# A new order of steps in a one-core kernel of a long convolution beside a gated feed-forward layer

## The chip, the cores and the metric

The kernel runs on one core of a Trainium2 chip. The metric is the device time of one execution in microseconds, taken as the median of several runs. The core has five engines with a queue of instructions each: TensorE (PE in the profile, its weight loads PEld), VectorE (DVE), ScalarE (ACT), GpSimd (POOL) and SyncE (SP), which in this kernel issues nearly all transfers. Each queue runs in order. An instruction that has to wait for another engine or a transfer holds up everything behind it on its own queue.

## The reference

```python
x = A_q                                  # (1, 2048, 640), bf16
xn = _layernorm(x, axis=-1)
# A: short convolution with 4 taps, gate, long convolution over the whole sequence
k_shift = sum over t of k_pad[:, t:t + S, :] * shift_k[:, 3 - t]
kv = k_shift * v
y = irfft(rfft(kv, 4096) * rfft(ssm_k, 4096))[:S]     # along the sequence
y = y + kv * ssm_D
A = xn * y
# B: gated feed-forward, 640 -> 1728 -> 640
h = _sigmoid(xn @ w_gate) * (xn @ w_up)
B = h @ w_down
return x + A + B
```

## The kernel before

The 2048 positions are laid on 128 partitions with 16 blocks each; the 640 channels are 5 chunks of 128. Two independent jobs share the core.

The feed-forward goes over four groups t of 512 positions. In each group there are 14 slices fc of the hidden width: `gate_mm` and `up_mm` (line 260, five matmuls each) write a PSUM tile, `gate_ev` (ScalarE, line 269) takes the sigmoid, and `up_ev` (VectorE, line 275) multiplies and writes `hT`. The last half-wide slice does both halves at once (`both_mm`, `both_ev`, `both_mul`, lines 281 to 290). Then come 16 `down_mm` steps of seven matmuls (line 304), and eight `down_ev` (VectorE, line 309) that add the result to `x`. For groups 1 to 3 the input is normalised on VectorE (`ln_norms`, `ln_var`, `ln_xn`, lines 198 to 219), with the inverse root on GpSimd (`ln_pow`, line 214), and turned by four DMA transpositions `xn_turn` into `xnT` (line 240). `xnT` is one buffer: the turns of a group wait for the last product of the group before, and the first `gate_mm` of a group waits for the turns.

The long convolution is done per chunk c as a Fourier transform in two stages by matrix products. The filter is turned on VectorE by `h_turn` (line 323) and its first element gets D added on GpSimd by `add_D` (line 317), which reads the one small buffer `dr`. VectorE forms the four-tap convolution and the gate in 16 `kv_op` steps (lines 337 to 346). `st1_mm` (lines 363 and 365, eight steps a chunk) is the first stage; `st1_ev` copies its PSUM tile into one of two `t1` buffers (`t` in the profile), and `wr1` writes a full one to DRAM (line 377). `rd2` reads it back in another layout (line 387), and `st2_mm` (line 396), `st2_ev` and `prod` (lines 409 and 411) do the second stage and the product with the filter. `inv1_mm` (line 425), `inv1_ev`, `wr2` (lines 441 and 445), `rdb` (line 455) and `inv2_mm` (line 464) transform back, and `inv2_q` and `inv2_x` (lines 469 and 474) multiply by `xn` and add to `x`.

PSUM is split into two pools. Pool `psG` has four tiles for gate, up, down and inv2 results; pool `psC` has two larger ones for st1, st2 and inv1. A matmul step that takes a tile waits for the eviction of the tile that had the buffer four (or two) steps before. The evictions of st1, st2 and inv1 go to ScalarE, or to VectorE where the order says so by one of the letters F, J and I in place of B, C and A.

The loads are steps as well: `load_k` and `load_halo` fill one of two K buffers (`kx`, chunk c uses number c modulo 2; the halo is the three columns ahead of the first), `load_v` one of two `kvh` buffers, `load_h` the filter `hn` and D's row `dr` (one buffer each, so it waits for `h_turn` and `add_D` of the chunk before), `load_taps` and `taps` the tap table, `load_x` the input of a group.

What runs when is written out by hand. Each kind of step is a chain with a letter, in its own fixed order, and one string names the chains in the order of issue:

```python
    left = {k: iter(v) for k, v in chains.items()}
    for k in "".join(ORDER.split()):
        fn, args = next(left[{"F": "B", "J": "C", "I": "A", "Y": "E"}.get(k, k)])
        fn(*args, **({"copy": dve_copy} if k in "FJIY" else {}))
```

Each engine sees its instructions in the order of this string. The letters that matter here: m, n the first loads and TB table; g all matmuls of the feed-forward; s and u their evictions; a, A, w stage 1, its eviction and its write-out; r, b, B, p stage 2; c, C, W, R, d, q the way back; k the short convolution; h, K, V, T the loads of later chunks; H, D the filter; l, P, e the normalisation and the turns; o the stores. Steps are numbered from 0 in the order of the string, 845 in all.

Of the kernel before, what the change touches and what calls it, by code (L numbers as in the profile page):

```python
# [57 lines left out]
def kernel(  # L58
# [569 lines left out]
    step("o", store, NB - 1, NB, 4 * P, DM)  # L628

    ORDER = """  # L630
    mgmmmmgmgmgsummZmgmgsmmgugmssgkmmukgskgugkusgsugkkgkHggmmuskuggkHmssukgmDgggukskgukkksaTmmgauAgmkaAH
    HlglAalAlglmwgautAkagugmggPmwlkgAhglkelauleggkakukkugekAAuuDkHgkuaaekgkwgsATKugkAwgsnkkgskgtuKaKAuka
    gskkgauwgkAlDAakVgglkKkrsakAuwAgakgVsAgalswAkaguKgkkAurbgkBswksHgTBgkbtuguBBpkgawkgslaAgsuKkalupKgrA
    AgkahPlnHsAwugaglVasgkgVpAsTAKukDpuckwglkkCgaCaHAugkAkgkeklubkgrkBBgguuwkgbggkpghtBBrbkegleBgBaauegw
    HAparguVkApauAkgwpADWaugakksAngkugpkwlAsucgsgJlpkCulbrgBKBsgaAuapgpAgrbsFggBussWkukrlpcHgguPCCgbslkV
    ggBuBgbpslBkuBRdpgspgWqqcusdgCgkrkkrCsbqFugqBgubskgBRdwBuagpAaqAdgllWwrsewRpugaqgIaggrpAaAaqupgIqupg
    ddcCgeuqgJebgupegFRuBgqbBpgqBgWpdcrguqqgJqCrubwuwdrgFpBgsbqpggpWpqBugBpscsuJggCurpgbggRFBbsWpdsudupq
    rgBqgqBcqRJsgrpCgsbBuWguBpdspqgbuBBgpqdpsgcgrugCRJqbpggsduBqsBgupgspgWqRqcuJdqgsgCdoqgusqWgudggqgugo
    uRgquRggddouqqgguqddgqqqqoquqggoogouoogouoooo
    """  # L640
    left = {k: iter(v) for k, v in chains.items()}
    for k in "".join(ORDER.split()):
# [33 lines left out]
```

## Time and profile before

| | us |
|---|---|
| median of 3 runs | 238.9 (238.31 to 239.72) |
| the profiled execution | 237.94 |
| its span, first to last instruction | 236.2 |
| TensorE busy | 229.1 (97%) |
| VectorE busy | 204.1 (86%) |
| ScalarE busy | 121.7 (52%) |
| DMA queue of SP, share of 16 engines | 90.3% |

The granted TensorE clock is at full speed throughout. Busy time of a matmul runs from its start to a modelled end, and matmuls overlap, so the sum over a group is larger than the time it takes from TensorE; the time from one start to the next (the pitch) is what counts. In the lists of waits the columns are the engine and line that waited, what ended the wait, the total in us, the number of waits and the longest one. In a timeline row they are the start and the duration in us, then engine, line, operation, what is written and read, and in brackets the idle time of the engine before it.

### The profile page before, as it was taken

The numbers are of one execution on the slowest core, as the hardware profiler recorded it, in microseconds if no ns is written. First come the engines' busy times: TensorE is split into PE (matmuls) and PEld (weight loads), VectorE is DVE, ScalarE is ACT, GpSimd is POOL, SyncE is SP. The second block draws the span as 40 slices with busy tenths as digits, with TensorE's granted clock in tenths as the row PEclk, the third lists the DMA queues.
The fourth block names the chain that finished last, engine by engine and source line by source line (L and its number), as shares of the span: only waits on it lengthen the run. The fifth ranks groups of instructions, "written<-read, shape, count | busy, mean of one in ns | idle before, by whom it ended". The sixth has DMA issues, their size and how long they took to land.

```text
span 236.2 us, 5433 instructions
## 1 busy us (share of the span) xinstructions
PE 229.1 (97%) x2205; PEld 131.2 (56%) x2205; DVE 204.1 (86%) x364; ACT 121.7 (52%) x152; POOL 11.5 (5%) x24
## 2 busy tenths in 40 slices
PE   7799999999899899999999999999999999999995
PEld 3664445877355445666754444478664344446772
DVE  3632898999969999999999999899999999988473
ACT  2343323633564897776776777653346367653000
POOL 5210000020100001000100010000000000000000
PEclk9999999999999999999999999999999999999999
DMA  6999999958899999899899996899989879556664
GB/s 211 292 313 237 259 308 299 257 174 163 223 317 269 321 253 270 225 286 217 228 232 321 248 265 186 240 246 271 235 260 284 238 186 255 160 155 177 191 212 134
DMA packets 97183, 56.79 MB, mean 240 GB/s; under 512 B 55878, under 2 KB 91270, under 8 KB 96902
## 3 DMA queue, kind: packets, MB, share of 16 engines
q1 hardware_dynamic: 96214, 55.62, 90.3%
q10 hardware_dynamic: 944, 0.82, 1.1%
q8 instruction: 17, 0.28, 0.5%
q14 instruction: 8, 0.07, 0.1%
HBM read 36.12 MB, written 18.35 MB: 231 GB/s over the span
## 4 chain that ended last, share of the span: by engine, by line
PE 84%; DVE 8%; DMA 4%; issue 1%; ACT 0%; ACTq 0%; DVEq 0%
PE pg L260 23%; PE pu L260 23%; PE pd L304 20%; PE psb L464 4%; PE ps L396 3%; DMA w<-in_B_w_up_dram 3%; PE ps L363 3%; PE ps L365 3%; PE psa L425 2%; PE pg L281 1%; DVE st L198 1%; DVE tmp L341 1%; DMA xnT<-xn 1%; DVE acc L343 1%; PE pu L251 1%
## 5 line engine op out<-in xcount | busy, mean ns | idle before, releaser
L260 PEld LDWEIGHTS <-w 128*128 128x128 bf16 x500 | 46.5, 98 | 55.8 <-issue 6.8
L304 PE MATMUL pd<-wd,hT 128*128 128x320 bf16 (+2 forms) x448 | 65.3, 299 | 0.0
L260 PE MATMUL pg<-xnT,w 128*128 128x512 bf16 x250 | 62.2, 380 | 0.9 <-DMA xnT<-xn 0.9
L260 PE MATMUL pu<-xnT,w 128*128 128x512 bf16 x250 | 62.2, 380 | 0.8 <-DVE hT L275 0.8
L304 PEld LDWEIGHTS <-hT 128*128 128x128 bf16 x448 | 41.9, 98 | 18.2 <-issue 2.3
L223 ACT CAST t<-ps 128x1024 bf16<-128x1024 f32 x38 | 37.8, 1016 | 23.6 <-PE ps L365 16.0
L269 ACT ACTIVATE sig<-pg 128x512 bf16<-128x512 f32 x52 | 31.1, 603 | 30.7 <-PE pg L260 27.7
L223 ACT CAST xz<-ps 128x1024 bf16<-128x1024 f32 x35 | 34.2, 1015 | 20.3 <-PE ps L396 20.3
L275 DVE TENSOR_TENSOR hT<-sig,pu 128x512 bf16<-128x512 bf16 x52 | 34.8, 675 | 9.6 <-PE pu L260 5.6
L411 DVE TENSOR_TENSOR xz<-xz 128x2048 bf16<-128x2048 bf16 x20 | 24.3, 1215 | 0.1
L365 PE MATMUL ps<-kvh,S1t 128*128 128x128 bf16 x160 | 21.7, 220 | 0.0
L363 PE MATMUL ps<-kvh,S1t 128*128 128x128 bf16 x160 | 21.6, 218 | 0.0
L341 DVE TENSOR_TENSOR tmp<-kx,sc 128x1024 bf16<-128x1024 bf16 x30 | 20.5, 683 | 0.4
L343 DVE TENSOR_TENSOR acc<-acc,tmp 128x1024 bf16<-128x1024 bf16 x30 | 20.5, 684 | 0.4
L309 DVE TENSOR_TENSOR x<-pd,x 128x320 bf16<-128x320 f32 (+2 forms) x32 | 15.2, 483 | 5.9 <-PE pd L304 5.7
L363 PEld LDWEIGHTS <-S1t 128*128 128x128 bf16 x160 | 15.5, 97 | 2.8 <-DVE kvh L346 0.3
L365 PEld LDWEIGHTS <-S1t 128*128 128x128 bf16 x160 | 15.4, 96 | 2.6
L198 DVE BATCH_NORM_STATS2 st<-x 128x6 f32<-128x320 bf16 x32 | 13.9, 476 | 2.7 <-DMA x<-in_A_q_dram 2.7
L469 DVE TENSOR_TENSOR yx<-psb,xn 128x512 bf16<-128x512 f32 x20 | 13.7, 684 | 1.4 <-PE psb L464 1.0
L409 DVE STREAM_SHUFFLE xz<-xz 128x512 f32<-128x512 f32 x20 | 14.5, 725 | 0.0
L223 ACT CAST ao<-psa 128x1024 bf16<-128x1024 f32 x11 | 10.8, 1014 | 5.8 <-PE psa L425 5.6
L464 PEld LDWEIGHTS <-TBt 128*128 128x128 bf16 x160 | 9.8, 98 | 3.0 <-issue 1.5
(48 smaller groups left out, 149.3 us busy)
## 6 DMA issues: line engine op xcount, KB each, us to landing
d<-t SPq DMA_DIRECT2D x20, 512.0 KB, 5.3
t<-d SPq DMA_DIRECT2D x20, 512.0 KB, 5.7
bi<-d SPq DMA_DIRECT2D x8, 512.0 KB, 4.8
d<-ao SPq DMA_DIRECT2D x6, 512.0 KB, 5.6
kx<-in_A_k_dram SPq DMA_DIRECT2D x10, 256.0 KB, 5.3
hn<-in_A_ssm_k_dram SPq DMA_DIRECT2D x20, 128.0 KB, 5.2
kvh<-in_A_v_dram SPq DMA_DIRECT2D x10, 256.0 KB, 5.4
x<-in_A_q_dram SPq DMA_DIRECT2D x3, 640.0 KB, 6.4
```

What stands on the lines that cost most here:

```text
L198: nc.vector.bn_stats(d["st"][:, i, s2, :], x[:, b, s2 * 320:(s2 + 1) * 320])
L223: nc.scalar.copy(out=out, in_=in_)
L260: nc.tensor.matmul(pg[:, :], lhsT=w[:, c, u * UP + fc * P:u * UP + (fc + 1) * P], rhs=xnT[:, :, c, :], start=(c == 0), stop=(c == NC - 1))
L269: nc.scalar.activation(sig[fc][:, :], pgs[0, fc][:, :], ACT.Sigmoid)
L275: nc.vector.tensor_tensor(hT[:, fc, :], sig[fc][:, :], pgs[1, fc][:, :], ALU.mult)
L304: nc.tensor.matmul(pd[:, :], lhsT=hT[:, fc, bb * P:(bb + 1) * P], rhs=wd[:, fc, es], start=(fc == 0), stop=(fc == NFC - 1))
L341: nc.vector.tensor_tensor(d["tmp"][:, :, :], kx[:, lo + 3 - m:hi + 3 - m, :], sb(m), ALU.mult)
L343: nc.vector.tensor_tensor(d["acc"][:, :, :], d["acc"][:, :, :], d["tmp"][:, :, :], ALU.add)
L363: nc.tensor.matmul(ps[:, i, 0:P], lhsT=S1[:, b, h, :], rhs=cin[c]["kvh"][:, 0, b, :], start=True, stop=True)
L365: nc.tensor.matmul(ps[:, i, P:2 * P], lhsT=S1[:, b, h, :], rhs=hp[:, b // 2, b % 2, :], start=True, stop=True)
L411: nc.vector.tensor_tensor(z[:, 1:3, :, :], z[:, 0:1, :, :].to_broadcast((P, 2, 8, P)), z[:, 1:3, :, :], ALU.mult)
L464: nc.tensor.matmul(ps[:, i, :], lhsT=TB[:, h, 4 * m + i, :], rhs=bi[:, h, 4 * (m % 2) + i, :], start=(h == 0), stop=(h == 1))
```

## The change

Only the string ORDER is replaced. All chains and all functions stay, so the same 845 steps are issued, each chain in its own order; what moves is how the chains are woven into each other. Fifteen evictions change their engine: seven go from VectorE to ScalarE and eight the other way, so that VectorE has 15 of them (letters F, I and J) instead of 14.

```diff
     step("o", store, NB - 1, NB, 4 * P, DM)
 
     ORDER = """
-    mgmmmmgmgmgsummZmgmgsmmgugmssgkmmukgskgugkusgsugkkgkHggmmuskuggkHmssukgmDgggukskgukkksaTmmgauAgmkaAH
-    HlglAalAlglmwgautAkagugmggPmwlkgAhglkelauleggkakukkugekAAuuDkHgkuaaekgkwgsATKugkAwgsnkkgskgtuKaKAuka
-    gskkgauwgkAlDAakVgglkKkrsakAuwAgakgVsAgalswAkaguKgkkAurbgkBswksHgTBgkbtuguBBpkgawkgslaAgsuKkalupKgrA
-    AgkahPlnHsAwugaglVasgkgVpAsTAKukDpuckwglkkCgaCaHAugkAkgkeklubkgrkBBgguuwkgbggkpghtBBrbkegleBgBaauegw
-    HAparguVkApauAkgwpADWaugakksAngkugpkwlAsucgsgJlpkCulbrgBKBsgaAuapgpAgrbsFggBussWkukrlpcHgguPCCgbslkV
-    ggBuBgbpslBkuBRdpgspgWqqcusdgCgkrkkrCsbqFugqBgubskgBRdwBuagpAaqAdgllWwrsewRpugaqgIaggrpAaAaqupgIqupg
-    ddcCgeuqgJebgupegFRuBgqbBpgqBgWpdcrguqqgJqCrubwuwdrgFpBgsbqpggpWpqBugBpscsuJggCurpgbggRFBbsWpdsudupq
-    rgBqgqBcqRJsgrpCgsbBuWguBpdspqgbuBBgpqdpsgcgrugCRJqbpggsduBqsBgupgspgWqRqcuJdqgsgCdoqgusqWgudggqgugo
-    uRgquRggddouqqgguqddgqqqqoquqggoogouoogouoooo
+    mmmmmmmmmggggsmmsumggsguuZsgggmukksmgmskmukgkggkmuksHgsggumkuggskgukHgskgmkmuggmkTsksgKuugkDagaAgkmA
+    uaHKtHmwmagllllAglgDPkAuaAwmklllahuelgekAugekakkugaggAgkggkAakaukuewgkukmkkgsTggAkuwsngkVutAgaskwkgs
+    AKgaukgrHkaAgAualakswkgAagVguskrAgAbgkwTksuBkBskkguKDgskkHlkaagguAlAKkngbtwushungpkplBsBgaAwgaugkpKl
+    gksaupgAAPlglswkVslrgkuKaueaglHAwaggkkAAVDcwCggTkaCkukuaAgregHkkAbggkugBBKkuurpbBgeklgBkgpbpgBluBpeg
+    atawAkuWggskuaklpghuAwasgAAgaarluAkHrkggAcVskgkJupgsCbgDswBugkBuspaAaKklgPgpAbugBkFsWrgRkcVCCsgugpdH
+    rsbpBkgBugWqudbsgplkpgrBBcurgqRCsqJgbgWkwgukgswpBrBlubksBFqgusludapdqaglgeAaguggRqAeaquAwAappgAaepqe
+    ggIcgCuwguJbBgpFdgrbpqugWBuqdpqBrgcugJpqgrCbugpsRwBFggpbupgBdsrqBuWpgdqrcJspggqgCbuFRqBggsubpdsWugBB
+    gdprscCqgpJrqgbsuBgqFRgupsgbspudpgqrWBgBduqqRcpgJCqWgsqbsBugBgpugsRdpgpucsgqJqCWdgqgusqgudgqouggudRq
+    gqugoRogggqudguodqgqqdudoggqqqqgogqoouuoooooo
     """
     left = {k: iter(v) for k, v in chains.items()}
     for k in "".join(ORDER.split()):
```

Places of the steps that the prediction speaks of, counted in the string:

| step | before | after |
|---|---|---|
| h_turn(0,1) | 64 | 68 |
| load_halo(2) | 176 | 86 |
| wr1(0,0) | 112 | 107 |
| load_k(2,0,8) | 193 | 103 |
| add_D(1) | 159 | 119 |
| ln_pow(1) | 126 | 120 |
| load_h(2) | 133 | 133 |
| xn_turn(1,0) to (1,3) | 137, 142, 153, 167 | 135, 138, 143, 166 |
| gate_mm(1,0) | 169 | 168 |
| load_v(1,8,16) | 127 | 172 |
| kv_op(2,0) | 198 | 195 |
| wr1(1,1) | 229 | 220 |
| up_ev(1,4) | 228 | 228 |
| st2_mm(0) | 255 | 235 |
| load_x(3) | 307 | 270 |
| load of the TB table | 429 | 279 |
| wr1(3,1) | 416 | 421 |
| inv1_mm(1) | 441 | 441 |

## The prediction

> **What bounds the kernel now.** First the page, for shares; then TensorE's waits; then, for each wait, the timeline around it and the waits of the engine that ended it.
>
> ```profile
> span 236.2 us, 5433 instructions
> PE 229.1 (97%) x2205; PEld 131.2 (56%) x2205; DVE 204.1 (86%) x364; ACT 121.7 (52%) x152; POOL 11.5 (5%) x24
> ```
>
> TensorE's busy share is overstated, because matmuls overlap. So I measured pitches, start to start: 1.08 us for a gate or up product (5 matmuls), 0.95 for seven down matmuls, 0.45 for an st1 or inv2 group, 0.47 for st2, 0.69 for inv1. The ordered steps then add up to 216.2 us of TensorE work. The first starts at 14.39 us and the last at 232.73; the last costs 0.39. 232.73 + 0.39 - 14.39 = 218.7, so TensorE loses only about 2.5 us in the whole order, and all that counts is in two places.
>
> ```profile
> PE pg L260 <- DMA xnT<-xn: 0.9, 1, 0.9
> PE pu L260 <- DVE hT L275: 0.8, 1, 0.8
> ```
>
> By pitch these are 1.10 us (the st1 group at 58.51 + 0.45 = 58.95, next product at 60.05) and 0.93 us (gate_mm(1,6) at 75.72 + 1.08 = 76.80, up_mm(1,6) at 77.73): 2.03 us, or 0.85% of the span. That is the most an order alone can win on TensorE; VectorE, 97% busy from 80 to 200 us (116.6 of 120), hides beside it.
>
> The first wait, in the timeline (start, duration, engine, line, tiles):
>
> ```profile
> 48.80 0.17 DVE L210 TENSOR_SCALAR var<-mv 128x4 f32<-128x4 f32 x1
> 49.11 1.02 POOL L214 TENSOR_TENSOR rstd<-var,mhalf 128x4 f32<-128x4 f32 x1 [17.25 <-DVE var L210]
> 50.10 0.42 POOL L317 TENSOR_TENSOR kvh<-kvh,dr 1x128 bf16<-1x128 bf16 x1
> 50.55 0.26 SPq L136 DMA_DIRECT2D dr<-in_A_ssm_D_dram  x1
> 50.90 2.35 SPq L139 DMA_DIRECT2D hn<-in_A_ssm_k_dram  x4
> 53.36 5.27 SPq L240 DMA_TRANSPOSE xnT<-xn  x4
> 60.05 1.24 PE L260 MATMUL pg<-xnT,w 128*128 128x512 bf16 x5 [0.93 <-DMA xnT<-xn]
> ```
>
> The first normalised block is ready at 50.84, but its transposition is issued only at 53.36: SP stands at load_h(2), which overwrites dr and so waits for add_D(1), and add_D(1) stands on POOL behind ln_pow. SP's own waits, cut to 40 to 82 us, price it:
>
> ```profile
> SPq L136 <- POOL kvh L317: 3.3, 1, 3.3
> ```
>
> The second wait comes from VectorE, which had lost time ten microseconds earlier:
>
> ```profile
> 69.21 0.69 DVE L337 TENSOR_TENSOR acc<-kx,sc 128x1024 bf16<-128x1024 bf16 x1 [1.73 <-DMA kx<-in_A_k_dram]
> 76.99 0.68 DVE L275 TENSOR_TENSOR hT<-sig,pu 128x512 bf16<-128x512 bf16 x1
> 77.73 1.24 PE L260 MATMUL pu<-xnT,w 128*128 128x512 bf16 x5 [0.77 <-DVE hT L275]
> ```
>
> kv_op(2,0) waited 1.73 us for K of chunk 2, issued at 62.16. up_ev(1,4), which frees the PSUM buffer for up_mm(1,6), ran late behind it.
>
> **The change, part by part.** All instructions stay; one eviction more goes to VectorE (15 against 14). Work ahead of a step is counted in pitches: VectorE 0.60 for a conv or up step, 1.03 a statistics block, 0.36 a normalisation, 0.40 a down_ev, 1.14 an eviction; ScalarE 0.91 an eviction.
>
> First wait, credit 1.10. add_D(1) now stands ahead of ln_pow on POOL, so load_h(2) no longer waits for it. SP comes from wr1(0,1), which waits for st1_ev(0,3) (st1_mm(0,2) arrives at 44.9, then taps(1) and two evictions on ScalarE: about 47.6), then load_v(1,0,8) (0.4), then load_h(2) with its 2.35: SP is free near 51.5. Against this, h_turn(0,1) now stands behind up_ev(0,10) and kv_op(0,9) and ends at about 36.4 instead of 34.7; load_h(1) waits for it, its data land near 43.5 (5.3 after the last issue, as before), and h_turn(1,0) starts 0.8 later than its 42.68. So ln_var ends at 49.75 and rstd at 50.9. Three VectorE steps (0.6 + 0.4 + 0.6) stand between, so ln_xn(1,0) runs at 51.35 and the first transposition at 51.8, the fourth three pitches of 1.35 later: 55.85 instead of 57.41. Landing moves from 60.0 to about 58.5. TensorE has the same 44.5 us ahead and arrives at 58.9. The wait closes with 0.4 to spare, which is all the cover that late x or hn data have.
>
> Second wait, credit 0.93. load_halo(2) and load_k(2,0,8) move from step 176 and 193 to 86 and 103, issued near 39 and 42, so kv_op(2,0) has its data 15 us early. up_ev(1,4) also moves forward: 47.4 us of VectorE work ahead instead of 49.6. With the 1.73 gone it starts near 76.99 - 2.2 - 1.7 = 73.1, and up_mm(1,6) arrives at 75.6. If the load's part failed, 2.2 alone would still bring it to 74.8.
>
> Debit: the t write-outs. Stage 1 is evicted into two t buffers, and ScalarE waits for the write d<-t before it fills one again; the trace shows such waits already, unseen by TensorE:
>
> ```profile
> ACT t L223 <- DMA d<-t: 6.9, 5, 2.6
> d<-t SPq DMA_DIRECT2D x20, 512.0 KB, 5.3
> ```
>
> The new order has three places where the same wait reaches TensorE through the two PSUM buffers. With L the write's time to land: (a) wr1(0,0) goes out at 45.2 (st1_mm(0,1) at 43.5, 0.6 for its rows, 1.0 to evict), st1_ev(0,4) ends 1.0 after it has landed, st1_mm(0,6) arrives at 51.4: stall L - 5.2. (b) wr1(1,1) at 69.7 (st1_mm(1,3) at 68.0, the same 1.6), then st1_ev(1,6) and (1,7) (0.91 + 1.0), and st2_mm(0), moved from 82.1 to 76.7: L - 5.1. (c) wr1(3,1) at 117.2 (st1_ev(3,3) stands behind gate_ev(2,0), free at 116.1), two evictions, inv1_mm(1) at 123.7: L - 4.6. At the median L of 5.3 this is 0.1 + 0.2 + 0.7 = 1.0. At these writes' own times before (4.1, 5.6, 2.9) it is 0 + 0.5 + 0 = 0.5. The bounds: nothing at 4.6 or less, 4.3 us at 6.4, the longest such write. I take 0.75, between the two near values, since the writes keep their places but not their neighbours.
>
> The extra eviction on VectorE (a 1.22 us row) I cost at nothing in the sum: VectorE's idle 3.4 us between 80 and 200 cover it. Other moved loads (x(3) from 88.6 to 75, the TB table from 118.5 to 83, V of chunk 1 to 48 and 57) have 1.5 us or more in hand by the same count. The end of the order keeps 3.4 us between the last matmul and the end of the span.
>
> Sum: -1.10 - 0.93 + 0.75 = -1.28 us. Profiled execution 237.94 (span 236.2 plus 1.74 around it): 236.7. The median of the runs shown, 238.9, lies 0.96 above the profiled one; I carry the difference over: 237.6.
>
> A row for traffic: DMA share is 1.24 between 42 and 46 us, at 269 GB/s, so the queue is full where the K loads now go. The Trainium skill (DMA: Bandwidth & Descriptors, section Queues, rings and completion order) says that on each DMA engine descriptors are consumed in ring order, so a load put ahead delays those behind. By it wr1(0,0) has 95 KB more ahead of it (the second halo), 0.35 us as an estimate at that rate, and the sum would be -0.93 instead of -1.28; no row here shows the order of service itself.
>
> **The rivals.**
>
> *Late write-outs* (slower). The mechanism of the debit, with L grown by the denser early traffic. The three stalls sum to 3L - 14.9; they eat the whole 2.03 from L = 5.6 on. At 6.4 they cost 4.3, net +2.3: 241.2. For it: the share over 1.1 at 66 to 70 and 74 to 82 us, and rows of tile t up to 7.5. Slower by over 1.2 from L = 6.05. Against: the median of 5.3, and V of chunk 1 leaving the burst around 44.
>
> *VectorE takes over.* It moves forward by the 1.73 it no longer waits, TensorE by 2.03, and it carries 1.2 more: it ends up as much as 1.5 later against TensorE than now. The nearest products had 0.75 in hand (prod(7,1) before inv1_mm(3)). So about 0.75 comes back on top of the debit, net -0.5: 238.4.
>
> *The first wait stays*, because x(1) or hn(1) land over 0.4 late: only 0.93 less 0.75, net -0.2: 238.7.
>
> *Nothing comes back*: L under 4.6 at all three places, net -2.0: 236.9.
>
> **How the numbers follow.** About 0.5% (1.2 us) is what a measurement of this kernel can tell from no change; the three runs before spread over 1.4. Chances: forecast 0.40 (0.34 of it beyond 0.5%), nothing comes back 0.10, VectorE 0.18, first wait stays 0.10 (0.03 of it slower, with a later landing still), late write-outs 0.22 (0.18 of it with L over 6.05). Faster 0.34 + 0.10 = 0.44; slower 0.18 + 0.03 = 0.21; the rest 0.35. The range runs from 0.6 below 236.9, just under half of what the runs scatter, to 240.2, which takes in the late write-outs up to L near 6.0.
>
> **What would show it.** Right: SP's 3.3 us wait for POOL gone, the first transposition near 52, no TensorE wait for xnT near 59, no 1.73 at kv_op(2,0), and small TensorE waits near 51, 77 and 124 on ScalarE's evictions. Wrong: a TensorE wait for xnT that stays, waits on VectorE's products between 130 and 165 us, or ScalarE waiting far over 6.9 us for d<-t.

## The result, and the profile after

| | before | after |
|---|---|---|
| median of 22 runs each, us | 239.08 (237.74 to 240.67) | 237.38 (236.36 to 238.75) |
| the profiled execution, us | 237.94 | 238.75 |
| its span, us | 236.2 | 236.9 |

The ratio of after to before is 0.993, with a 95% interval of 0.991 to 0.995: 1.7 us faster. Forecast were 237.6 us and 1.28 us less. The two profiled executions differ the other way: that of after is the slowest of its 22 runs, and only one of the 22 runs of before is below the profiled 237.94. The spans must not be subtracted; what is read below are single waits and places, and a second profiled execution of after (label a2_after, 236.94 us, span 235.1) is used beside the first.

Two of the rows of TensorE's waits in after:

```profile
PE ps L396 <- DMA t<-d: 1.4, 1, 1.4
...
PE psa L425 <- ACT t L223: 0.2, 1, 0.2
```

Neither line of the two waits of before is left: at line 260 TensorE waits neither for `xnT` nor for `hT`. Shares of busy time do not tell the kernels apart (TensorE 97% in both, VectorE 86% before and 87% after, ScalarE 52% and 51%). Both waits shown are new, 1.4 us at a second-stage product and 0.2 us at an `inv1_mm`; they are followed up below.

The first wait, in the timeline of after:

```profile
48.67 0.97 SPq L136 DMA_DIRECT2D dr<-in_A_ssm_D_dram  x1
49.15 0.17 DVE L210 TENSOR_SCALAR var<-mv 128x4 f32<-128x4 f32 x1
49.46 1.33 POOL L214 TENSOR_TENSOR rstd<-var,mhalf 128x4 f32<-128x4 f32 x1 [4.83 <-DVE var L210]
49.74 1.86 SPq L139 DMA_DIRECT2D hn<-in_A_ssm_k_dram  x4
50.83 1.16 DVE L219 TENSOR_SCALAR xn<-x,mv,rstd 128x640 bf16<-128x640 bf16 x3
51.71 5.83 SPq L240 DMA_TRANSPOSE xnT<-xn  x4
59.16 1.24 PE L260 MATMUL pg<-xnT,w 128*128 128x512 bf16 x5
```

SP issues D's row at 48.67, ahead of the end of `ln_pow` (50.79), where before it stood until 50.55; SP has no wait for POOL any more. The first transposition goes out at 51.71 instead of 53.36, and the product starts at 59.16 without an idle time in brackets.

The second wait, in the timeline of after: `kv_op(2,0)` (line 337), `up_ev(1,4)` (line 275) and `up_mm(1,6)` (line 260):

```profile
65.31 0.69 DVE L337 TENSOR_TENSOR acc<-kx,sc 128x1024 bf16<-128x1024 bf16 x1
72.47 0.69 DVE L275 TENSOR_TENSOR hT<-sig,pu 128x512 bf16<-128x512 bf16 x1
76.13 1.24 PE L260 MATMUL pu<-xnT,w 128*128 128x512 bf16 x5
```

The 1.73 us in brackets are gone (K of chunk 2 landed at 46.25), and up_mm(1,6) does not wait.

### The profile page after: what moved, and what is told of

Its sections match the earlier page's. It is cut to its first block, busy times and chain, and to the rows that moved or that the text cites. A ratio compares the mean times of both kernels' runs of the same rounds, so it can differ in the third digit from the quotient of the medians.

```text
span 236.9 us, 5443 instructions
## 1 busy us (share of the span) xinstructions
PE 230.2 (97%) x2205; PEld 132.0 (56%) x2205; DVE 205.7 (87%) x365; ACT 120.4 (51%) x151; POOL 12.7 (5%) x24
## 4 chain that ended last, share of the span: by engine, by line
PE 70%; DVE 13%; DMA 11%; issue 2%; ACT 2%; SPq 0%; ACTq 0%; DVEq 0%
PE pu L260 20%; PE pg L260 20%; PE pd L304 14%; DMA d<-t 5%; PE psb L464 3%; PE ps L396 3%; DMA t<-d 3%; DMA w<-in_B_w_up_dram 3%; PE psa L425 3%; DVE acc L343 2%; PE ps L363 2%; PE ps L365 2%; DVE tmp L341 2%; DVE x L309 1%; DVE st L198 1%
## 5 line engine op out<-in xcount | busy, mean ns | idle before, releaser
L304 PE MATMUL pd<-wd,hT 128*128 128x320 bf16 (+2 forms) x448 | 66.0, 299 | 0.0
L304 PEld LDWEIGHTS <-hT 128*128 128x128 bf16 x448 | 41.8, 98 | 18.4 <-issue 2.3
L223 ACT CAST t<-ps 128x1024 bf16<-128x1024 f32 x39 | 38.4, 1014 | 17.2 <-PE ps L365 13.7
L223 ACT CAST xz<-ps 128x1024 bf16<-128x1024 f32 x34 | 33.2, 1014 | 17.0 <-PE ps L396 14.4
L363 PE MATMUL ps<-kvh,S1t 128*128 128x128 bf16 x160 | 21.3, 217 | 0.1
L365 PE MATMUL ps<-kvh,S1t 128*128 128x128 bf16 x160 | 21.3, 219 | 0.0
L223 ACT CAST ao<-psa 128x1024 bf16<-128x1024 f32 x10 | 9.9, 1013 | 8.9 <-PE psa L425 7.8
L464 PEld LDWEIGHTS <-TBt 128*128 128x128 bf16 x160 | 10.3, 98 | 3.1 <-issue 0.5
```

The lines of the kernel that those rows point to most:

```text
L223: nc.scalar.copy(out=out, in_=in_)
L304: nc.tensor.matmul(pd[:, :], lhsT=hT[:, fc, bb * P:(bb + 1) * P], rhs=wd[:, fc, es], start=(fc == 0), stop=(fc == NFC - 1))
L363: nc.tensor.matmul(ps[:, i, 0:P], lhsT=S1[:, b, h, :], rhs=cin[c]["kvh"][:, 0, b, :], start=True, stop=True)
L365: nc.tensor.matmul(ps[:, i, P:2 * P], lhsT=S1[:, b, h, :], rhs=hp[:, b // 2, b % 2, :], start=True, stop=True)
L464: nc.tensor.matmul(ps[:, i, :], lhsT=TB[:, h, 4 * m + i, :], rhs=bi[:, h, 4 * (m % 2) + i, :], start=(h == 0), stop=(h == 1))
```

## The experiments

Each run is compared with runs of the kernel before that were made beside it on the same chip. In the diffs only the pieces of the string are shown that differ; `...` stands for what is left out.

**One half of the idea alone, on the old order.** Two kernels take only the two moves that the prediction paid for, one each, and a third both. Nothing else of the new string is in them.

e1_pool: add_D(1) (`D`) ahead of ln_pow(1) (`P`).

```diff
-    ...ggPmwlkg...AAuuDkHg...
+    ...ggDPmwlkg...AAuukHg...
```

> The old order with one step moved: add_D(1) ahead of ln_pow(1) on GpSimd. Theory (the gain is the two TensorE waits at 59 and 77 us): SP no longer waits 3.3 us for POOL, the first transposition goes out near 51 instead of 53.4, the xnT wait of 1.1 us goes. VectorE is not earlier, but SP reaches the K loads of chunk 2 earlier, so the wait at up_mm(1,6) may stay or shrink: -0.2 to -1.1 us against before. Rival (the gain lies in the reweaving of everything after 80 us): no change, within 0.2 us.

Measured: 237.15, ratio 0.9929 (0.9897 to 0.996), 1.9 less, more than expected. TensorE's waits in its profile at the ordered products:

```profile
PE ps L363 <- DVE kvh L346: 0.5, 1, 0.5
PE ps L363 <- ACT sc L151: 0.2, 1, 0.2
PE pu L260 <- DVE hT L275: 0.2, 1, 0.2
```

and `kv_op(2,0)` in its timeline:

```profile
60.69 2.78 SPq L155 DMA_DIRECT2D kx<-in_A_k_dram  x2
67.87 0.69 DVE L337 TENSOR_TENSOR acc<-kx,sc 128x1024 bf16<-128x1024 bf16 x1 [1.02 <-DMA kx<-in_A_k_dram]
```

The wait for `xnT` is gone, and the other one shrank from 0.93 to 0.31 us by pitch, although its loads kept their place in the string: SP, free earlier, issued K at 60.69 instead of 62.16. The two waits are coupled, and 1.10 was too little for this move: by pitch the two waits together shrank by 1.7 us.

e2_kload: load_halo(2) and load_k(2,0,8) (`K`) to the places where K's buffer has just come free.

```diff
-    ...ksaTmmgauAgmkaAH...gsATKugk...tuKaKAuka
+    ...ksaTKmmgauAgKmkaAH...gsATugk...tuaKAuka
```

> The old order with load_halo(2) and load_k(2,0,8) moved ahead of the K loads of chunk 1. Theory: kv_op(2,0) no longer waits 1.7 us, the TensorE wait of 0.9 us at up_mm(1,6) goes, the xnT wait near 59 us stays or grows by a few tenths since more traffic goes ahead: -0.5 to -0.9 us. Rival (gain lies after 80 us): no change, within 0.2 us.

Measured: 237.52, ratio 0.9945 (0.9916 to 0.9973), 1.6 less (0.65 to 2.0 by the interval), also more than expected. The wait on `hT` is gone, and the wait for `xnT` stays, with SP's wait for POOL:

```profile
PE pg L260 <- DMA xnT<-xn: 1.2, 1, 1.2
...
SPq L136 <- POOL kvh L317: 1.4, 1, 1.4
```

e3_both: both moves on the old order.

```diff
-    ...ksaTmmgauAgmkaAH...ggPmwlkg...AAuuDkHg...gsATKugk...tuKaKAuka
+    ...ksaTKmmgauAgKmkaAH...ggDPmwlkg...AAuukHg...gsATugk...tuaKAuka
```

> The old order with both moves (add_D(1) ahead of ln_pow(1), first K loads of chunk 2 early), nothing else. Theory: both TensorE waits go, 2.0 us less what comes back later: -1.2 to -2.0 us, at least as much as the whole new order gained (-1.7). Rival (gain lies in the rest of the reweaving): half of it or less, above -0.8 us. Second rival (the closed waits open again at the next place): TensorE waits of 1 us or more at new places in the profile.

Measured: 236.34, ratio 0.99 (0.9862 to 0.9939), 2.75 less, again more than expected. Between its first and its last product one line of TensorE waits is left in its profile:

```profile
PE ps L363 <- ACT sc L151: 0.2, 1, 0.2
```

So three steps moved in the old string bring more than the whole new string does, and more than the 2.03 us of the two waits. Where the other 0.5 to 0.7 us come from was not found; the profiled execution of before is itself 1 us below its median, so a usual run of before has losses that its profile does not show. It was run again (e7_both2) beside the new order (a2_after).

> The old order with both moves, once more beside the new order on the same chip. Theory (the two moves are the whole gain, the rest of the reweaving costs): 0.5 to 1.3 us faster than the new order, -2.0 to -2.8 us against before. Rival (the first run of it was lucky): within 0.3 us of the new order.

> The new order as it is, once more, for a second profile. Theory (what the new order gives back is the wait of st2_mm(4) for rd2(4), which has no time in hand there and lands between 4.0 and 7.5 us after its issue): the profile shows this wait again between 0 and 1.6 us, and no other TensorE wait over 0.5 us. Rival (VectorE's extra eviction): TensorE waits on VectorE between 130 and 165 us that sum to more than the wait at st2_mm(4). Time: -1.4 to -2.0 us against before.

Measured on one chip: 236.43 (236.19 to 237.17, 6 runs) for the two moves, ratio 0.9892 (0.9858 to 0.9927); 237.36 (236.87 to 238.63, 12 runs) for the new order, ratio 0.9936 (0.9912 to 0.996). The intervals touch, but all runs of the first lie below the median of the second. The new order gives back about 0.9 us. The profiled execution of e7_both2, the slowest of its six, has three small waits of TensorE where that of e3_both has one: 0.5 us for `kvh`, 0.4 for `xz` and 0.3 for `xnT`. So the first wait is closed there with nothing to spare.

**The moves taken back, out of the new order.** If the two moves carry the gain, undoing them should cost it.

e6_pool_undo: only `D` and `P` change places.

```diff
-    ...AglgDPkAua...
+    ...AglgPDkAua...
```

> The new order with add_D(1) behind ln_pow(1) on GpSimd again, all else kept. Theory: SP waits for POOL again (2 to 3.5 us), the transpositions go out 1.5 to 2 us later, TensorE waits for xnT near 59 us by 0.8 to 1.6 us, and the time is 0.8 to 1.6 us over the new order. Rival (the early K loads alone matter): within 0.3 us of the new order.

Measured: 238.89, ratio 0.9999 (0.9973 to 1.0025), 1.5 over the new order that was run beside it: two letters hold nearly all of the new order's gain. Its timeline repeats the old chain, POOL to SP to the transpositions to TensorE:

```profile
49.30 1.33 POOL L214 TENSOR_TENSOR rstd<-var,mhalf 128x4 f32<-128x4 f32 x1 [17.89 <-DVE var L210]
50.61 0.43 POOL L317 TENSOR_TENSOR kvh<-kvh,dr 1x128 bf16<-1x128 bf16 x1
51.06 0.26 SPq L136 DMA_DIRECT2D dr<-in_A_ssm_D_dram  x1
...
53.95 5.26 SPq L240 DMA_TRANSPOSE xnT<-xn  x4
60.72 1.24 PE L260 MATMUL pg<-xnT,w 128*128 128x512 bf16 x5 [1.54 <-issue]
```

The releaser of the last row is given as "issue"; but the transpositions go out from 53.95, 2.24 us later than in after, and the swap of the two letters is the only difference.

e10_k_undo: only the two loads go back, behind load_taps(2) and load_x(2).

```diff
-    ...mkTsksgKuugk...uaHKtH...gsTggAkuwsng...
+    ...mkTsksguugk...uaHtH...gsTKggAkuwsnKg...
```

> The new order with only the first K loads of chunk 2 taken back (load_halo(2) behind load_taps(2), load_k(2,0,8) behind load_x(2)); add_D(1) stays early. Theory (both waits count by themselves): kv_op(2,0) waits 1 to 3 us for K, TensorE waits 0.5 to 1.5 us between 70 and 80 us, time 0.4 to 1.5 us over the new order. Rival (up_ev(1,4) moved forward covers it, so the early K loads bring nothing here): within 0.3 us of the new order.

Measured: 240.78, ratio 1.0098 (1.0059 to 1.0136). That is 3.4 over the new order's median on other chips, well over what was expected. Part of this may be the clock: six of its ten runs show a granted clock of 0.993, and the four at 1.0 (239.27 to 241.0) lie 1.9 to 3.6 over the new order. The profiled execution is one of these four, and two rows of its timeline say why, the first of `kv_op(2,0)`, the second of a stage 1 eviction:

```profile
70.00 0.69 DVE L337 TENSOR_TENSOR acc<-kx,sc 128x1024 bf16<-128x1024 bf16 x1 [4.53 <-DMA kx<-in_A_k_dram]
...
73.48 1.01 ACT L223 CAST t<-ps 128x1024 bf16<-128x1024 f32 x1 [2.98 <-DMA d<-t]
```

and TensorE's waits:

```profile
PE ps L363 <- ACT t L223: 2.0, 1, 2.0
```

VectorE waits 4.53 us, not 1.73, because the new order reaches `kv_op(2,0)` earlier and the loads no earlier (issued at 62.53). And wr1(1,0), issued at 67.02 while K was moving, landed only about 73.4, 6.4 us later; in a2_after it was issued at 66.25 and the same eviction ran at 71.01 after a wait of 1.19. That is the mechanism of the rival of the late write-outs; in the new order the same eviction holds TensorE by only 0.2 to 0.4 us.

e5_undo: both taken back, the second load a little later still than in e10, behind st1_mm(1,2).

```diff
-    ...mkTsksgKuugk...uaHKtHmwmagllllAglgDPk...gsTggAkuw...Agaskwkgs
+    ...mkTsksguugk...uaHtHmwmagllllAglgPDk...gsTKggAkuw...AgKaskwkgs
```

> The new order with the two moves taken back: add_D(1) behind ln_pow(1), the first K loads of chunk 2 behind load_taps(2) and at st1_mm(1,2). Theory: the xnT wait near 59 us comes back (0.8 to 1.3 us), the wait at up_mm(1,6) only in part, since up_ev(1,4) has 2.2 us less work ahead: time within 0.7 us of the old order. Rival (gain lies in the rest): stays within 0.4 us of the new order, so 1.3 us or more under the old one.

Measured: 244.1, ratio 1.0217 (1.017 to 1.0263), 5.0 over the old order where 0.7 at most was expected, and 6.7 over the new one, so the steps were not independent. `kv_op(2,0)`'s load was issued at 65.00, behind four transpositions that had been held up by POOL:

```profile
PE ps L363 <- ACT t L223: 2.2, 1, 2.2
PE pg L260 <- DMA xnT<-xn: 2.0, 1, 2.0
...
DVE acc L337 <- DMA kx<-in_A_k_dram: 7.5, 1, 7.5
```

With these three steps where e5 has them, the rest of the new string is far worse than the old one.

**Where the 0.9 us went.** The first suspect was the new TensorE wait at st2_mm(4), for rd2(4). In e4_st2late, st1_mm(3,2) and (3,3) with their evictions go ahead of it, as cover (and `taps(4)`, which stands between them).

```diff
-    ...lgBkgpbpgBluBpegatawAkuWggskuaklpghuAwasg...
+    ...lgBkgaAtppgaAlupegbBBwkuWggskuaklpghuwasg...
```

> The new order with the two stage-1 steps st1_mm(3,2) and (3,3) and their evictions ahead of st2_mm(4), so that st2_mm(4) comes 1.9 us of down products and 0.9 us of stage 1 later. Theory: the wait for rd2(4) goes, 0.3 to 1.2 us faster than the new order, near the old order with both moves. Rival (VectorE or the rest): within 0.2 us of the new order.

Measured: 237.25, ratio 0.9934 (0.9909 to 0.996): the same as the new order. The wait is not the steady cost. The two profiled executions of the new order show it: rd2(4) and the product that reads it, first in after, then in a2_after.

```profile
105.66 1.62 SPq L387 DMA_DIRECT2D t<-d  x1
...
113.20 0.14 PEld L396 LDWEIGHTS <-SMt 32*32 32x32 bf16 x16 [1.72 <-DMA t<-d]
```

```profile
105.75 0.37 SPq L387 DMA_DIRECT2D t<-d  x1
...
111.84 0.43 PE L396 MATMUL ps<-t,SMt 32*32 32x512 bf16 x16
```

Issued at the same time, the transfer took 7.5 us in one and 4.75 in the other; this costs TensorE 1.4 us or nothing.

Then the string was cut in two at both_mm(1). e8_newhead has the new order up to there and the rest in the old sequence; e9_newtail has the old order with both moves up to there and the rest in the new sequence.

```diff
-    [new head, steps 0 to 311] [new tail]
+    e8: [new head] [the remaining steps in the old sequence]
+    e9: [old head with both moves] [the remaining steps in the new sequence]
```

> The new order up to its both_mm(1) (step 311, near 94 us), then all steps left in the sequence of the old order. Theory (the new head closes the waits, the new tail costs about 1 us against the old tail): like the old order with both moves, 236.2 to 236.8, so -2.2 to -2.8 us against before. Rival (the new head itself costs the 1 us, by traffic or by its evictions): 237.2 to 237.7, like the new order.

> The old order with both moves up to its both_mm(1), then all steps left in the sequence of the new order. Theory (the new tail costs about 1 us): 237.2 to 237.7, like the new order. Rival (the new head costs it): 236.2 to 236.8, like the old order with both moves.

Measured: e8 237.48, ratio 0.9953 (0.993 to 0.9976); e9 237.23, ratio 0.995 (0.9927 to 0.9973). For e9 that is the forecast, for e8 it is the rival. By their ratios both stand by the new order (0.993 and 0.9936), or a little above it, and not by the two moves alone (0.99 and 0.9892), so neither half holds the loss by itself. The seams add waits of their own (0.8 us at line 425 in e8, for an eviction), so this cut does not settle it.

What the profiles do show is three small losses that come with one string or one half of it. From the start of the last matmul step to the end of the span it is 3.64 to 3.66 us in all seven profiles that have the new tail (after, a2_after, e4, e5, e6, e9, e10), and 3.44 to 3.45 in the seven that have the old one: 0.2. The new string ends in six stores behind the last down_ev, the old one in four, and the last store is issued 0.28 us after VectorE's end (a2_after) against 0.07 (before). And the first ordered product starts at 14.42 to 14.76 us with the new head, at 14.09 to 14.39 with the old one: about 0.2 more, cause not found.

The third is a stop inside a step, which the lists of waits do not show, because busy time runs to a modelled end. In a2_after TensorE begins st2_mm(19), loads three of its 16 weights, and goes on 0.34 us later, when VectorE has ended `inv1_ev(8,0)`. The new string gives this eviction to VectorE (letter J), which does three other steps first; the old string gives it to ScalarE (C) and `inv1_ev(8,1)` to VectorE.

```profile
204.21 1.21 DVE L226 CAST ao<-psa 128x1024 bf16<-128x1024 f32 x1
205.13 0.09 PEld L396 LDWEIGHTS <-SMt 32*32 32x32 bf16 x3 [0.42 <-issue]
205.47 0.13 PEld L396 LDWEIGHTS <-SMt 32*32 32x32 bf16 x13 [0.25 <-issue]
```

The same loss, 0.33 to 0.34 us by pitch, stands in all seven profiles with the new tail and in none with the old one. The three losses make about 0.75 of the 0.9 us. Waits for the write-outs of t, told below, come on top of them; against them stand small waits of the order with the two moves. No run puts one of them right by itself, so these shares are read from traces and not shown by an experiment.

**A second profile of before.** e11_before is the old order once more.

> The old order as it is, for a second profile. Theory: the same two TensorE waits, 0.7 to 1.4 us before gate_mm(1,0) and 0.6 to 1.3 us before up_mm(1,6), and no other over 0.5 us. Rival (the first profile was an odd one): one of them is missing.

Measured: 238.38. Both waits are there again, with their sizes:

```profile
PE pu L260 <- DVE hT L275: 0.9, 1, 0.9
PE pg L260 <- DMA xnT<-xn: 0.8, 1, 0.8
```

They belong to the order, not to one execution.

## Why the prediction was right, and where it was not

**First wait, credit 1.10.** Right in cause and in place; e1 and e6 show it from both sides. The chain ran close to the forecast: h_turn(0,1) ended at 36.60 (36.4), `ln_var` at 49.3 (49.75), the root at 50.8 (50.9), first transposition at 51.71 (51.8), product at 59.16 (58.9). Two steps erred against each other: load_h(1) landed at 41.8, not 43.5, and the transpositions were issued 1.54 us apart, not 1.35 (the fourth at 56.32 against 55.85). The size of the credit was too small: taken alone on the old order, the move brought 1.9 us (1.0 to 2.5 by its interval); SP's freed time also brought K's loads forward, and with them 0.6 us of the second wait.

**Second wait, credit 0.93.** Right: e2 closes it alone, with a gain of 1.6 us whose interval takes in 0.93, and in after up_ev(1,4) ran at 72.47 (73.1), up_mm(1,6) at 76.13 (75.6), without a wait. Wrong was the sentence that the move of up_ev by 2.2 us would do it even if the load's part failed (74.8): in e10 up_ev(1,4) ran only at 76.90, because VectorE's time ahead of `kv_op(2,0)` is not gained when the data are late; it turns into a longer wait for them.

**Debit 0.75.** This term had the right mechanism at the wrong places. At the three places that it names, the writes landed faster than the 5.3 us that were assumed, or the eviction waited for something else. In after, st1_ev(0,4) started 4.2 us after wr1(0,0) was issued, and it waited for TensorE, not for the write; wr1(1,1) landed after 4.9 us and wr1(3,1) after 3.6. By the stalls as written this is nothing at all three, the small waits that were announced near 51, 77 and 124 us are not there, and ScalarE's own wait fell instead of growing:

```profile
ACT t L223 <- DMA d<-t: 3.4, 3, 1.8
```

But writes of t reach TensorE at two other places. `st1_ev(1,4)` waits for wr1(1,0), 4.7 us after its issue, and holds st1_mm(1,6), in a2_after by 0.4 us by pitch (first row), in after by 0.2. `st1_ev(4,6)` waits for wr1(4,0) and holds inv1_mm(4), which the new string has close behind it, in after by 0.5 us with a stop inside the step (the other two rows), in a2_after by 0.1.

```profile
72.08 0.22 PE L363 MATMUL ps<-kvh,S1t 128*128 128x128 bf16 x1 [0.24 <-ACT t L223]
```

```profile
164.53 1.01 ACT L223 CAST t<-ps 128x1024 bf16<-128x1024 f32 x1 [1.84 <-DMA d<-t]
165.59 0.94 PE L425 MATMUL psa<-xz,SMt 32*32 32x512 bf16 x32 [0.19 <-ACT t L223]
```

That these come to 0.5 and 0.75 us, near the debit, is luck: none of it stands where the debit was worked out. Three more things were carried over unchanged or put at nothing, and were not nothing: the end (0.2), the start (0.2) and the change of eviction engines (0.34 at st2_mm(19)). rd2(4) fell under "other moved loads have 1.5 us or more in hand" and was never counted by name; it cost 1.4 us in one of two executions.

**The sum.** Measured side by side, the two moves alone bring 2.5 us and the new order 1.55: the credits of 2.03 were short by 0.45 and the debit of 0.75 by 0.2. The sum of -1.28 came out near what was measured partly because these two errors offset each other.

**The rivals.** *Late write-outs*: in the new order only the 0.5 to 0.75 us above; e10 and e5 show the mechanism at full size, with 2.0 and 2.2 us of TensorE, once K's loads are queued just ahead of wr1(1,0). *VectorE takes over*: in a2_after the list of waits has none of TensorE on VectorE between 130 and 165 us, and VectorE is busy 115.54 of 120 us between 80 and 200, against 116.55 before. VectorE does hold TensorE later, the 0.34 us at st2_mm(19), through an eviction that changed its engine. *The first wait stays*: it does not. *Nothing comes back* (236.9): e3 and e7 (236.34 and 236.43) come nearest to it, not the new order.

**The ring order.** By the Trainium skill (DMA: Bandwidth & Descriptors, section Queues, rings and completion order) the 95 KB of the second halo ahead of wr1(0,0) would have delayed it by an estimated 0.35 us and made the sum -0.93. The trace of after shows no such delay, but it shows only that the write took at most 4.2 us, since the eviction that needs it waited for TensorE; before it took 4.1. In the old string with K's early loads ahead of this write (e2, e3, e7, e9) the eviction does wait for it and starts 5.1 to 5.4 us after its issue, where without them (before, e1, e11) the write landed after 3.6 to 4.1, though in after the same loads stand ahead of it and it took no more than the 4.2. In e10 the write behind K's loads took 6.4 us against 4.8 in a2_after. The e-runs agree with the rule's sign; no run shows the order of service itself.

## What to carry to other kernels

A 0.4 us step on an almost idle engine can hold a queue of transfers and, by it, the busiest engine: look at what the issuing queue waits for, not at the busy shares. Try the few moves that the profile names on the old order first; here three moved letters beat a new weave of all 845 steps by about 0.9 us, and show which part of it pays. When moves share a queue their prices do not add: undone alone they cost 1.5 and 3.4 us (the latter partly at a lower clock), and 6.7 us together, with one load a little later still. And a list of waits can miss a stop inside a step: look at the rows of a step, too.

## What was not expected of the hardware

The same transfer in the same program, issued within 0.1 us of the same time, landed after 4.75 us in one execution and after 7.5 in another, and its issue on SP took 0.37 and 1.62 us. The median landing of the 20 writes d<-t was 5.3 us in the profile of before, 4.9 in that of after and 5.9 in a2_after. Runs of one kernel spread over 2.4 to 2.9 us, more than the whole effect, and one profiled execution can lie at either end; that the scatter of landings is what spreads them was not shown.
